# Query, key and value loads in partition halves, and attention products in 64x64 tiles, in a fused linear-attention and expert kernel

## The chip, the cores and the metric

The kernel runs on one core of a Trainium2 chip. The metric is the time of one execution on the device in microseconds (us), shorter is better. A core has a matrix engine (TensorE, "PE" in the profile, with its weight loads as "PEld"), VectorE ("DVE"), ScalarE ("ACT"), GpSimd ("POOL") and SyncE ("SP"), which here only issues transfers. Each engine runs its own instructions in order and waits on semaphores for the others. Data comes from main memory (HBM) by DMA into SBUF, which has 128 partitions; TensorE writes its products into PSUM, eight banks of 2 KB in each partition.

## The reference

Inputs are q, k and v of shape (4, 8, 768, 64): 4 batches, 8 heads, 768 tokens, 64 channels; a decay `lam` for each head; and the weights of an expert layer. All are float32.

```python
def _attn_ref(q, k, v, lam):
    block = 64
    ...
    Dmask = np.where(rel >= 0, lam[:, None, None] ** rel[None, :, :], 0.0)
    ...
    for b in range(nb):
        ...
        intra = np.einsum('bhic,bhjc->bhij', qb, kb) * Dmask[None]
        intra = np.einsum('bhij,bhjd->bhid', intra, vb)
        inter = np.einsum('bhid,bhde->bhie', qb * lam_pow[None], kv_state)
        out[:, :, sl] = intra + inter
        ...
        kv_state = lam_block[None, :, None, None] * kv_state + np.einsum('bhsd,bhse->bhde', kb_dec, vb)
    return out.astype(np.float32)

def _moe_ref(x, w_in, w_out, alpha):
    h = x @ w_in
    s = np.sin(alpha * h)
    g = h + s * s / (alpha + 1e-09)
    return (g @ w_out).astype(np.float32)
```

The attention's output, with the heads side by side, is the expert layer's x: 3072 tokens of 512 features. `w_in` is 512 x 2048 and `w_out` is 2048 x 512. Decay makes this linear attention: a token sees the tokens of its own block through masked scores, and all earlier ones of its batch through a state of 64 x 64 for each head.

## The kernel before, in words

**A planner.** The kernel doesn't write its instructions directly. Each step is given to `op(...)` with an engine (or a choice of engines), a guessed duration, and the names of the buffers that it reads and writes. `_Plan` puts the steps into an order of time by those guesses: SP's steps stay in the order given, TensorE's may be moved within a window of 40 steps, the others go to whichever engine would be done first. It then emits every engine's instructions with semaphore waits. `P.lead` moves a step ahead in that order. So the text sets the dependences and roughly the order, and the guessed durations set the rest.

**Blocks and chunks.** Tokens go in blocks of 128, which are 6 to a batch (`NB`) and 24 in all (`NBLK`). Four blocks make a chunk of 512 tokens (`TCH`), and there are 6 chunks.

**Attention of a block.** `load_q` brings q of two blocks (two tokens a run, 512 bytes), `load_kv` brings k and v of one block (one token a run, 256 bytes); all loads go through `load` (L340) on SP's queue. They are float32, with the 128 tokens of a block on the 128 partitions. `scale_block` multiplies q and k by powers of the decay (`Lq`, `Lk`; L459 and L466, mostly on POOL) into `qk2`, and copies v to bfloat16 (`v2`, L468). `piece_Q` and `piece_T` transpose q and k on TensorE for the first 12 blocks (`TD = 12`; L501 and L483), with copies out of PSUM into `qkT`; later blocks are transposed by a DMA on SP's queue (L474). `part_S` makes the scores in 64x64 tiles of the array (L536), and DVE multiplies them by the mask into `Sm` (L545). `part_O` adds two things in one PSUM bank: the carried state `Zc` times q, in 64x64 tiles (L590), and v times `Sm`, 128 tokens deep in 128x64 tiles (L597); its copy into `xT` (L606) is the transposed input of the expert layer. `part_Z` adds k times v into the state, also 128 deep (L561), in a bank of its own (`ZB`) that gathers through a batch; a copy to bfloat16 follows (L569). `run` joins such parts into one step of TensorE, and `piece_G` joins the scores of one block with the output and state of the block before.

**Expert layer.** `unit_A` makes 128 of the 2048 hidden features for a chunk, with four products of 128x512 (L645); ACT takes the sine (L655), POOL or ACT squares it (L660 or L659), and DVE adds it up into `gT` (L662). `unit_A2` does the same for two groups of 128 features and half a chunk (L679 to L697). `unit_B` makes a quarter of the sum over the hidden features for 128 tokens, with four products (L710); the last quarter is followed by a copy (L723) and a store (L725). The first quarter of `w_in` comes in float32 over SP's queue (`ws`) and is cast by DVE (L389); the other three and all of `w_out` come over GpSimd's queue with a cast in the transfer (L376 and L395 call `load`). The first of these waits for the last k of the first four blocks (`last["k32", 3]`); block 4's q waits for the weight load `last["w1", 2]`.

**Order.** Blocks 0 to 3 are done first, in pieces that are written out one by one. TensorE has little else then, and `spin` fills its gaps with products that nobody reads. Chunk 0's units A follow, then a written-out mixture of pieces of blocks 4 to 11, units B of chunk 0 and units A of chunk 1. From chunk 2 on a loop puts a unit A of chunk c beside a unit B of chunk c-1 and a joint attention run at five or four places of the sixteen.

Of the kernel before, what the change touches and what calls it, by code (L numbers as in the profile page):

```python
# [243 lines left out]
def bass_lightning_attn__then__act_snake_kernel(  # L244
# [34 lines left out]
    with es:  # L279
# [18 lines left out]
        q32 = ring("q32", RL // 2, [128, H, 2, D], F32)  # L298
        k32 = ring("k32", RL, [128, H, D], F32)
        v32 = ring("v32", RL, [128, H, D], F32)  # L300
        qk2 = sb("qk2", [128, R2, 2 * H, D], BF16)
        v2 = ring("v2", R2, [128, H, D], BF16)
        qkT = sb("qkT", [128, RT, 8, 128], BF16)
        Sm = ring("Sm", 2, [128, 8, 128], BF16)
        Zc = ring("Zc", 2, [128, 4, D], BF16)
        mask = sb("mask", [128, 8, 128], BF16)
        maskf = sb("maskf", [128, 128], F32)
        ident = sb("ident", [128, 128], BF16)
        identf = sb("identf", [128, 128], F32)
        lam_bc = sb("lam_bc", [128, H], F32)  # L310
        lnlam = sb("lnlam", [128, H], F32)
        E_i = sb("E_i", [128, 2 * NB, H], I32)
        E_f = sb("E_f", [128, 2 * NB, H], F32)
        lnL = sb("lnL", [128, 2 * NB, H], F32)
        Lq = sb("Lq", [128, NB, H], F32)
        Lk = sb("Lk", [128, NB, H], F32)
# [11 lines left out]
        def _(_unused_eng):  # L328
# [4 lines left out]
            op = P.op  # L333
            P.EARLY = 20.0, 0.3
# [8 lines left out]
            def load_q(s, after=()):  # L343


                b, n, j = s // NB, s % NB, s // 2 % (RL // 2)
                for lo, hi in ((0, 4), (4, H)) if s < 4 else ((0, H),):
                    last["q32", s] = load(
                        q32[j][:, lo:hi, :, :].rearrange("p h t d -> p h (t d)"),
                        q[b, lo:hi, n * BL:(n + 2) * BL, :].rearrange("h (p t) d -> p h (t d)", t=2),  # L350
                        [("q32", j, a) for a in range(lo // 4, hi // 4)],
                        (0.9 if s == 0 else 1.1 if s < 4 else 2.3), f"q32{j}" + (str(lo) if s < 4 else ""),
                        lat=2.7, after=after, runs=8 * (hi - lo),
                    )

            def load_kv(s, which="kv"):
                b, n, j = s // NB, s % NB, s % RL
                for nm, src, dst in (("k32", k, k32), ("v32", v, v32)):
                    if nm[0] in which:
                        last[nm, s] = load(  # L360
                            dst[j][:, :, :],
                            src[b, :, n * BL:(n + 1) * BL, :].rearrange("h p d -> p h d"),
                            (nm, j), 1.1, f"{nm}{j}", lat=2.7,
                        )

            def load_pair(s):
                load_q(s)
                load_kv(s)
                load_kv(s + 1)
# [16 lines left out]
            def cast_w1_first():  # L386
                for lo in (0, 256):
                    op("DVE",
                       lambda e, lo=lo: (e.copy if e is nc.scalar else e.tensor_copy)(  # L389
                           w1[:, :, lo:lo + 256], ws[:, :, lo:lo + 256]), 0.7, [("ws", lo)], [("w1", lo // 256)])  # L390

            def load_w2(i, after):
# [7 lines left out]
            load(lam_bc[:, :], bass.AP(lam.tensor, 0, [[0, 128], [1, H]]), "lam", 0.1, "lam", "ACT", runs=1)  # L400
            load(alphaT[:, :], bass.AP(moe_alpha.tensor, 0, [[128, NM], [1, 128]]), "alphaT", 0.1, "alphaT", "ACT", lat=4.9, runs=1)
            load_q(0)
            load_kv(0, "k")
            load_kv(1, "k")
            load_kv(0, "v")
            load_kv(1, "v")
            load_q(2)
            load_kv(2, "k")
            load_kv(3, "k")
            load_kv(2, "v")  # L410
            load_kv(3, "v")

            op("POOL", lambda e: e.iota(E_i[:, 0:NB, :], [[256, NB // 2], [1, 2], [0, H]], base=0,
                                        channel_multiplier=2), 0.6, writes=["E_i"])
            op("POOL", lambda e: e.iota(E_i[:, NB:2 * NB, :], [[128, NB], [0, H]], base=0, channel_multiplier=1),
               0.6, writes=["E_k"])
            op("POOL", lambda e: e.tensor_copy(E_f[:, :, :], E_i[:, :, :]), 0.3, ["E_i", "E_k"], ["E_f"])
# [7 lines left out]
                out=maskf[:, :], in_=maskf[:, :], pattern=[[1, 2], [2, 64]], compare_op=ALU.is_ge,  # L425
                fill=0.0, base=0, channel_multiplier=-1), 0.5, ["maskf"], ["maskf"])
            op("DVE", lambda e: e.tensor_copy(mask[:, :, :], bass.AP(maskf, 0, [[128, 128], [0, 8], [1, 128]])),
               0.8, ["maskf"], ["mask"])

            op("ACT", lambda e: e.activation(lnlam[:, :], lam_bc[:, :], ACTF.Ln), 1.5, ["lam"], ["lnlam"])  # L430
            lnlam_b = bass.AP(lnlam, 0, [[H, 128], [0, 2 * NB], [1, H]])
            op("DVE", lambda e: e.tensor_tensor(lnL[:, :, :], E_f[:, :, :], lnlam_b, ALU.mult), 0.2,
               ["E_f", "lnlam"], ["lnL"])
            op("ACT", lambda e: e.activation(Lq[:, :, :], lnL[:, 0:NB, :], ACTF.Exp), 0.3, ["lnL"], ["Lq"])
            op("ACT", lambda e: e.activation(Lk[:, :, :], lnL[:, NB:2 * NB, :], ACTF.Exp, scale=-1.0), 0.3,
# [10 lines left out]
            def QE(s, a):  # L446
                return "DVE" if (s, a) in () else "POOL"

# [4 lines left out]
            def scale_block(s):  # L453
                n, jl, j = s % NB, s % RL, s % R2
                lk = bass.AP(Lk, n * H, [[NB * H, 128], [1, H], [0, D]])
                jq = s // 2 % (RL // 2)
                for a in range(2) if s % 2 == 0 else ():
                    ported(op(QE(s, a),
                       lambda e, a=a: e.tensor_tensor(  # L459
                           qk2[:, j:j + 2, 4 * a:4 * a + 4, :],  # L460
                           q32[jq][:, 4 * a:4 * a + 4, :, :].rearrange("p h t d -> p t h d"),
                           bass.AP(Lq, n * H + 4 * a, [[NB * H, 128], [H, 2], [1, 4], [0, D]]), ALU.mult),
                       1.05 if QE(s, a) == "POOL" else 0.7,
                       [("q32", jq, a), "Lq"], [("q2", j, a), ("q2", j + 1, a)]))
                ported(op("DVE" if s in (0,1) else "POOL",
                   lambda e: e.tensor_tensor(qk2[:, j, H:2 * H, :], k32[jl][:, :, :], lk, ALU.mult), 0.7 if s in (0,1) else 1.05,  # L466
                   [("k32", jl), "Lk"], [("k2", j)]))
                op((("ACT", 0.62, 0.0), ("POOL", 1.05, 0.3)) if s > 11 else "ACT", lambda e: (e.copy if e is nc.scalar else e.tensor_copy)(v2[j][:, :, :], v32[jl][:, :, :]), 0.62,  # L468
                   [("v32", jl)], [("v2", j)])

            def piece_T(s, tb):
# [8 lines left out]
                def mm(e):  # L480
                    ins = None
                    for jp in range(4):
                        ins = e.transpose(tp[:, jp, :], qk2[:, j, H + 2 * jp:H + 2 * jp + 2, :], ident[:, :])  # L483
# [25 lines left out]
            def run(*parts, after=()):  # L509
# [4 lines left out]
                def mm(e):  # L514
                    ins = None
                    for p in parts:
                        ins = p[0](e)
# [386 lines left out]
```

## Time and profile before

| | us |
|---|---|
| median of 3 runs | 223.47 (223.21 to 226.68) |
| span of the profiled execution | 221.6 |
| TensorE busy | 205.4 |
| ACT busy | 154.1 |
| DVE busy | 119.5 |
| POOL busy | 89.2 |

The span reaches from the first to the last instruction of the core; the time of a run holds some 1.9 us more than that span. TensorE's granted clock is full (1.00) in all of it. Matmuls are pipelined: a 128x512 product is listed with 379 ns, of which 216 pass until the next one starts.

The largest groups, with busy time and the mean of one:

| line, engine, what | count | us | ns each |
|---|---|---|---|
| L710 PE, expert output | 381 | 90.9 | 370 |
| L645 PE, expert hidden, 512 tokens | 290 | 73.2 | 379 |
| L679 PE, expert hidden, 256 tokens | 176 | 22.3 | 273 |
| L536 PE, scores | 384 | 10.3 | 229 |
| L597 PE, v times scores | 192 | 10.2 | 229 |
| L590 PE, state times q | 160 | 8.0 | 218 |
| L561 PE, state update | 160 | 6.1 | 201 |
| L545 DVE, mask | 24 | 29.2 | 1222 |
| L459 POOL, scale of q | 24 | 25.0 | 1062 |
| L466 POOL, scale of k | 22 | 22.9 | 1044 |

By queue, SP's moved 76,880 packets with 24.25 MB, GpSimd's 3,696 with 3.67 MB, and ACT's 3,056 with 5.13 MB. The loads of k and of v are 24 each of 256 KB; those of q are 10 of 512 KB and 4 of 256 KB.

### The profile page before, as it was taken

To read this page: it belongs to the slowest core of one execution; us is meant where nothing else is said; L and a number is where in the kernel's file an instruction comes from. 1 tells how busy PE (TensorE), PEld (TensorE's weight loads), DVE (VectorE), ACT (ScalarE), POOL (GpSimd) and SP (SyncE) were. 2 spreads that over 40 slices of the span, in tenths; PEclk is the share of its full clock that TensorE was granted. 3 is DMA by queue.
4 is the path that set the end of the run, shared out by engine and by line. 5 is a ranking of instruction groups with operands and counts; after the bars stand their busy time and mean duration, and the time that the engine had idled before them with its cause. 6 is when DMAs were issued, how large, how long until landed. Compare 5 with 4: busy or idle time off the path is not lost.

```text
span 221.6 us, 4485 instructions
## 1 busy us (share of the span) xinstructions
PE 205.4 (93%) x1850; PEld 111.1 (50%) x1877; DVE 119.5 (54%) x179; ACT 154.1 (70%) x272; POOL 89.2 (40%) x98
## 2 busy tenths in 40 slices
PE   4687998899899998999999999999999999999995
PEld 1365433456576775545445444545545444444444
DVE  2687676254688867666545464645465544445100
ACT  3644995347697995879788877776777677778211
POOL 2485765344895985945550733011001011110100
PEclk9999999999999999999999999999999999999999
DMA  5999999999999999999999950110110011101212
GB/s 131 234 232 273 207 212 210 204 239 239 214 263 282 240 165 243 203 270 188 276 219 239 216 124 18 50 47 3 47 47 30 20 47 47 50 0 47 76 68 98
DMA packets 83653, 33.35 MB, mean 150 GB/s; under 512 B 63520, under 2 KB 80688, under 8 KB 83632
## 3 DMA queue, kind: packets, MB, share of 16 engines
q1 hardware_dynamic: 76880, 24.25, 54.0%
q0 software_dynamic: 3696, 3.67, 9.9%
q10 hardware_dynamic: 3056, 5.13, 6.4%
q8 instruction: 15, 0.25, 0.5%
q14 instruction: 6, 0.05, 0.1%
HBM read 27.28 MB, written 6.29 MB: 151 GB/s over the span
## 4 chain that ended last, share of the span: by engine, by line
PE 60%; DMA 18%; SPq 12%; POOL 4%; ACT 3%; issue 2%; DVE 1%
PE bank L710 29%; PE bank L645 23%; SPq L340 12%; DMA v<-in_v_dram 8%; DMA w<-in_moe_w_in_dram 4%; DMA q<-in_q_dram 3%; PE bank L679 3%; DMA k<-in_k_dram 3%; PE bank L597 2%; PE bank L536 2%; PE bank L590 1%; POOL qk L466 1%; POOL qk L459 1%; POOL u L694 1%; DVE gT L697 1%
## 5 line engine op out<-in xcount | busy, mean ns | idle before, releaser
L710 PE MATMUL bank<-w,gT 128*128 128x512 bf16 (+1 forms) x381 | 90.9, 370 | 2.2 <-issue 1.7
L662 DVE SCALAR_TENSOR_TENSOR gT<-u,rinv,bank 128x512 bf16<-128x512 bf16 x74 | 54.6, 746 | 54.1 <-ACT u L659 34.5
L645 PE MATMUL bank<-xT,w 128*128 128x512 bf16 x290 | 73.2, 379 | 0.9 <-DVE gT L662 0.4
L655 ACT ACTIVATE t<-bank,alpha 128x512 bf16<-128x512 f32 x74 | 50.5, 686 | 24.4 <-PE bank L645 24.4
L710 PEld LDWEIGHTS bank<-w,gT 128*128 128x128 bf16 x400 | 37.7, 98 | 39.5
L660 POOL TENSOR_TENSOR u<-t 128x512 bf16<-128x512 bf16 x21 | 21.8, 1041 | 82.0 <-ACT t L655 81.1
L645 PEld LDWEIGHTS bank<-xT,w 128*128 128x128 bf16 x296 | 28.5, 98 | 34.6 <-DVE gT L662 0.8
L545 DVE TENSOR_TENSOR Sm<-bank,mask 128x1024 bf16<-128x1024 f32 x24 | 29.2, 1222 | 9.8 <-PE bank L561 7.1
L659 ACT ACTIVATE u<-t 128x512 bf16<-128x512 bf16 x53 | 33.1, 628 | 1.6
L459 POOL TENSOR_TENSOR qk<-q,Lq 128x512 bf16<-128x512 f32 x24 | 25.0, 1062 | 19.6 <-DMA q<-in_q_dram 15.2
L466 POOL TENSOR_TENSOR qk<-k,Lk 128x512 bf16<-128x512 f32 x22 | 22.9, 1044 | 7.6 <-DMA k<-in_k_dram 7.5
L679 PE MATMUL bank<-xT,w 128*128 128x256 bf16 x176 | 22.3, 273 | 2.7 <-DVE gT L697 2.0
L723 ACT COPY osb<-bank 128x512 f32<-128x512 f32 (+1 forms) x25 | 14.2, 569 | 14.7 <-PE bank L710 14.6
L697 DVE SCALAR_TENSOR_TENSOR gT<-u,rinv,bank 128x256 bf16<-128x256 bf16 x44 | 19.0, 476 | 7.8 <-POOL u L694 4.3
L689 ACT ACTIVATE t<-bank,alpha 128x256 bf16<-128x256 f32 x44 | 18.5, 472 | 3.5 <-PE bank L679 2.9
L679 PEld LDWEIGHTS bank<-xT,w 128*128 128x128 bf16 x176 | 16.2, 98 | 6.3 <-DVE gT L697 3.4
L468 ACT CAST v<-v 128x512 bf16<-128x512 f32 x20 | 12.2, 615 | 8.8 <-DMA v<-in_v_dram 8.6
L606 ACT CAST xT<-bank 128x512 bf16<-128x512 f32 (+1 forms) x18 | 12.9, 715 | 2.8 <-PE bank L561 1.4
L694 POOL TENSOR_TENSOR u<-t 128x512 bf16<-128x512 bf16 x11 | 11.3, 1039 | 5.7 <-ACT t L689 5.6
L536 PEld LDWEIGHTS bank<-qkT 64*64 64x64 bf16 x384 | 6.5, 110 | 8.4 <-issue 3.2
L536 PE MATMUL bank<-qkT 64*64 64x128 bf16 x384 | 10.3, 229 | 0.5 <-ACT qkT L506 0.3
L597 PE MATMUL bank<-Sm,v 128*64 128x128 bf16 x192 | 10.2, 229 | 0.5 <-DVE Sm L545 0.5
(50 smaller groups left out, 102.6 us busy)
## 6 DMA issues: line engine op xcount, KB each, us to landing
k<-in_k_dram SPq DMA_DIRECT2D x24, 256.0 KB, 5.6
v<-in_v_dram SPq DMA_DIRECT2D x24, 256.0 KB, 5.5
q<-in_q_dram SPq DMA_DIRECT2D x10, 512.0 KB, 5.5
out_dram<-osb ACTq DMA_DIRECT2D x19, 256.0 KB, 2.1
w<-in_moe_w_out_dram POOLq DMA_DIRECT2D x4, 512.0 KB, 13.3
w<-in_moe_w_in_dram POOLq DMA_DIRECT2D x3, 512.0 KB, 9.3
q<-in_q_dram SPq DMA_DIRECT2D x4, 256.0 KB, 4.5
ws<-in_moe_w_in_dram SPq DMA_DIRECT2D x2, 512.0 KB, 6.6
```

What stands on the lines that cost most here:

```text
L340: return op(eng, lambda e: e.dma_start(dst, src), dur, dma=sem, lat=lat, after=after, issue=issue, runs=runs, writes=key if isinstance(key ...
L459: lambda e, a=a: e.tensor_tensor(qk2[:, j:j + 2, 4 * a:4 * a + 4, :], q32[jq][:, 4 * a:4 * a + 4, :, :].rearrange("p h t d -> p t h d"), b ...
L466: lambda e: e.tensor_tensor(qk2[:, j, H:2 * H, :], k32[jl][:, :, :], lk, ALU.mult), 0.7 if s in (0,1) else 1.05,
L536: ins = e.matmul(ps[(b0, b1)[h]][w, 128 * jp:128 * (jp + 1)].rearrange("p (t x) -> p t x", x=64), qkT[r, jt, 4 + jp, w], qkT[r, jq:jq + 2, ...
L545: op("DVE", lambda e: e.tensor_tensor(Sm[s % 2][:, :, :], banks[:, 512 * b0:512 * b0 + 1024].rearrange("p (c i) -> p c i", i=128), mask[:, ...
L645: ins = e.matmul(ps[hb][:, c0:c1], w1[:, kc, 128 * m:128 * (m + 1)], xT[x][:, kc, c0:c1], start=(kc == 0 and c0 == lo), stop=(kc == NKC - ...
L655: op("ACT", lambda e: e.activation(t16[ju][:, w], ps[hb][:, w], ACTF.Sin, scale=alpha[:, m:m + 1]), 0.69 * f, [bank(hb), "alpha"], [("t16" ...
L659: lambda e: (e.activation(u16[ju][:, w], t16[ju][:, w], ACTF.Square) if e is nc.scalar else e.tensor_tensor(u16[ju][:, w], t16[ju][:, w], ...
L660: e.tensor_tensor(u16[ju][:, w], t16[ju][:, w], t16[ju][:, w], ALU.mult)), 0,
L662: op("DVE", lambda e: e.scalar_tensor_tensor(out=gT[g][:, m, w], in0=u16[ju][:, w], scalar=rinv[:, m:m + 1], in1=ps[hb][:, w], op0=ALU.mul ...
L679: ins = e.matmul(ps[hb][:, 256 * i:256 * i + 256], w1[:, kc, 128 * (m + i):128 * (m + i + 1)], xT[x][:, kc, lo:lo + 256], start=(kc == 0 a ...
L710: ins = e.matmul(ps[ob][:, w], gT[g][:, m, 128 * s4:128 * (s4 + 1)], w2[:, m, w], start=(m == 0), stop=(m == NM - 1),)
```

## The change

q, k and v of a block are loaded alike now. `load_x` makes six transfers of 128 KB a block: for each of the three, heads 0 to 3 go to partitions 0 to 63 and heads 4 to 7 to partitions 64 to 127, with two neighbouring tokens in one run of 512 bytes. So a partition holds a pair of tokens for four heads. The factors, the mask and the layouts of `qk2`, `v2` and `Sm` follow that. Products over the tokens of a block are 64 deep now and come in twos (even and odd tokens), so v times scores has 16 products for 8, and the state update 16 for 8; scores and state times q keep 16 and 8. All are in 64x64 tiles. The new `run` puts the scores of a block and the output and state of the block before into one step, dealt out over the four tiles by a guess of 56 and 32 ns a product. Products of both row halves add into the same bank; between those of the one and of the other stands a wait of TensorE on a semaphore of its own (`turn`), with scores placed ahead of it. The output takes two half banks: one is the second half of the state's bank (`ZB`), which DVE therefore sets to zero after each copy (`WIPE`). Transposes on TensorE take q and k of one block into one bank with one copy out.

Besides: the first weight load on GpSimd's queue waits for the last v of block 3; half of the cast of `ws` is on ACT; the first four units A each do half a chunk; the banks are dealt out anew; blocks 0 to 3 and 4 to 12 have a new written-out order, in which no output run stands alone before the last block; and the joint runs of the later chunks stand at places 2, 6, 10 and 13.

```diff
-            def load_q(s, after=()):
...
-            def load_kv(s, which="kv"):
...
+            def load_x(s, which="qkv", after=()):
...
+                b, n, j = s // NB, s % NB, s % RL
+                for x in which:
+                    for r in range(2):
+                        last[x, s] = load(
+                            x32[x][j][half(r), :, :, :].rearrange("p h t d -> p h (t d)"),
+                            {"q": q, "k": k, "v": v}[x][b, 4 * r:4 * r + 4, n * BL:(n + 1) * BL, :].rearrange(
+                                "h (p t) d -> p h (t d)", t=2),
+                            (x + "32", j, r), 0.47, f"{x}32{j}{r}", lat=2.7, after=after, runs=16,
                         )
...
-            load(lam_bc[:, :], bass.AP(lam.tensor, 0, [[0, 128], [1, H]]), "lam", 0.1, "lam", "ACT", runs=1)
+            for r in range(2):
+                load(lam_bc[half(r), :], bass.AP(lam.tensor, 4 * r, [[0, 64], [1, 4]]), ("lam", r), 0.1, f"lam{r}", "ACT", runs=1)
...
+            for s in range(4):
+                load_x(s)
...
+            def run(S=None, O=None, Z=None, b0=3, ob=2, ob2=None, parted=False, after=()):
...
+                if O is not None:
+                    for t in range(2):
+                        for r, u, w in RUW:
+                            first.append((r, w, 56, (obs[r], w), out_of(r, u, w),
+                                          v2[O % R2][half(r), 2 * u + w, t, :], Sm[O % 2][half(r), u, 2 * w + t, :]))
+                if O is not None and O % NB:
+                    for r, u, w in RUW:
+                        (first if r == u else then).append(
+                            (u, w, 56, (obs[r], w), out_of(r, u, w).rearrange("p (t x) -> p t x", t=2),
+                             Zc[O % 2][half(u), 2 * r + w, :], q_of(O, r, u, w)))
+                if Z is not None:
+                    for t in range(2):
+                        for r, u, w in RUW:
+                            (first if r else then).append(
+                                (r, u, 32, (ZB, u), ps[ZB][half(u), 64 * (2 * r + w):64 * (2 * r + w) + 64],
+                                 qk2[half(r), Z % R2, 1, 2 * w + t, u, :], v2[Z % R2][half(r), 2 * u + w, t, :]))
...
+                full = max(lanes.values()) + 110
...
+                    for i, (_, _, _, key, d, w, x) in enumerate(first + early + then):
+                        if first and then and i == len(first + early):
+                            e.wait_ge(turn, turns[0])
+                        ins = e.matmul(d, w, x, start=key not in begun, stop=True, skip_group_check=True)
+                        begun.add(key)
+                        if first and then and i == len(first) - 1:
+                            turns[0] += 1
+                            ins.then_inc(turn, 1)
...
+                    if ob2 is None:
+                        op(WIPE, lambda e: e.memset(ps[ZB][:, 256:512], 0.0), 0, [("xT", c % RX, i4, 2)], [bank(ZB)])
...
             for i in range(1, 4):
-                load_w1(i, [last["k32", 3]])
+                load_w1(i, [last["v", 3]])
...
+            FIRST = ("T4 G4 T5 G5 BBB BBB T6 G6 BBB T7 BBB G7 "
+                     "0 0 T8 0 0 G8 B 1 1 T9 1 B 1 G9 A T10 B A G10 A B A T11 A A G11 A A G12")
...
-                    if block <= NBLK and m in ((2, 6, 8, 11, 13) if c == 2 else (2, 7, 10, 13)):
...
+                    if block <= NBLK and m in (2, 6, 10, 13):
+                        attend("G", block)
                         block += 1
```

More of the change, by code (lines that the diff above doesn't have):

```diff
@@ new lines, in piece_T, with mm @@
+                for i, x in ((1, "k"), (0, "q")) if s == 0 else ((0, "q"), (1, "k")):
+                    def mm(e, i=i):
+                        ins = None
+                        for w in range(4):
+                            ins = e.transpose(tp[:, 4 * i + w, :], qk2[:, j, i, w, :, :], ident[:, :])
+                        return ins
+                    op("PE", mm, 0.3, [(x + "2", j), "ident"], [bank(tb)])
+                op((("DVE", 0.7, 0.0), ("ACT", 1.1, 0.0)),
+                   lambda e: (e.copy if e is nc.scalar else e.tensor_copy)(qkT[:, jt, :, :], tp),
+                   0, [bank(tb)], [("qT", jt), ("kT", jt)])
@@ L628, in _, with piece_G @@
+            def piece_G(s, t, ob=2):
+                run(S=s, O=t, Z=t, ob=ob)
             seen = [0]
@@ L847, in _ @@
+            assert ai == 16 and not stores, (ai, bi)
+            block = TD + 1
             for c in range(2, NCH):
```

476 lines of the change are left out of this document (196 added, 280 removed).

## The prediction

> **What bounds the kernel now.** I read the busy table and the slices first.
>
> ```profile
> PE 205.4 (93%) x1850; PEld 111.1 (50%) x1877; DVE 119.5 (54%) x179; ACT 154.1 (70%) x272; POOL 89.2 (40%) x98
> ...
> PE   4687998899899998999999999999999999999995
> ...
> DMA  5999999999999999999999950110110011101212
> ```
>
> TensorE is the bound from the fourth slice on, and the DMA engines are full for the first 115 us. The stretches say where the one waits for the other (columns: stretch, length, then busy us and instructions of each engine, clock, DMA share, GB/s).
>
> ```profile
> 0.00:20.70 20.70, 13.76 (x188) 8.11 (x190) 12.92 (x22) 10.61 (x18) 11.78 (x20) 1.00 1.03 218
> 20.70:45.00 24.30, 22.23 (x123) 10.63 (x127) 14.05 (x23) 15.93 (x27) 13.32 (x14) 1.00 1.16 207
> 45.00:87.00 42.00, 39.61 (x543) 27.79 (x548) 30.27 (x54) 32.00 (x69) 29.69 (x31) 1.00 1.09 235
> 87.00:125.00 38.00, 36.99 (x356) 18.93 (x361) 22.05 (x31) 31.68 (x56) 21.15 (x22) 1.00 1.20 234
> 125.00:204.00 79.00, 77.89 (x565) 37.52 (x573) 38.74 (x51) 60.09 (x96) 12.26 (x12) 1.00 0.15 47
> ```
>
> The expert products start only at 20.69; behind 87 us TensorE never rests, so there only fewer TensorE cycles help. Between, it idles a little. The chain of waits gives the reason for the late start: the issues on SP's queue, then the landing of k, then the expert weights.
>
> ```profile
> 0.81 0.45 SPq L340
> ...
> 1.32 0.48 SPq L340
> ...
> 9.14 5.70 DMA k<-in_k_dram
> ...
> 14.90 1.04 POOL qk L466
> 15.95 0.88 POOL w L340
> 16.82 9.34 DMA w<-in_moe_w_in_dram
> ```
>
> TensorE's timeline shows one joint attention run of now, and three stalls of the middle stretch.
>
> ```profile
> 38.92 0.40 PE L501 MATMUL bank<-ident,qk 128*128 128x128 bf16 x4 [0.75 <-POOL qk L459]
> ...
> 43.80 0.40 PE L483 MATMUL bank<-ident,qk 128*128 128x128 bf16 x4 [0.81 <-POOL qk L466]
> ...
> 59.54 1.05 PE L679 MATMUL bank<-xT,w 128*128 128x256 bf16 x8 [0.90 <-DVE gT L697]
> ...
> 98.85 0.42 PE L536 MATMUL bank<-qkT 64*64 64x128 bf16 x16
> 99.10 0.39 PE L590 MATMUL bank<-qkT,Zc 64*64 64x128 bf16 x8
> 99.42 0.41 PE L597 MATMUL bank<-Sm,v 128*64 128x128 bf16 x8
> 99.67 0.29 PE L561 MATMUL bank<-v,qk 128*64 128x64 bf16 x8
> 100.12 1.67 PE L645 MATMUL bank<-xT,w 128*128 128x512 bf16 x7 [0.16 <-issue]
> ```
>
> The profiled span is 221.6 us; the median of the runs, 223.47, is 1.9 above it. I sum against the span and add 1.9.
>
> **Loads at the start.** The completion records of the first four blocks give the pace of 256 KB: q (512 B runs) lands 0.95 to 0.98 us behind its forerunner (4.95 to 5.93, 11.48 to 12.43); k and v (256 B runs) 1.16 on average (5.93 to 10.58 for four, 12.43 to 17.07 for four). After, all have 512 B runs, but as twice as many transfers of 128 KB, each into half the partitions. No transfer of the trace is of that kind. Bounds: 0.95 per 256 KB, if halves run as whole ones of equal runs, and 1.9, if a half takes as long as a whole one. SP sets a floor: starts of unblocked issues lie 0.51 to 0.54 apart (0.81, 1.32, 1.85, 2.40), so 1.04 for two. I take p = 0.98, the nearest row. With 5.93 for the first two, the last load lands at 5.93 + 10p = 15.7, not 17.07.
>
> What waits for it moves: the first GpSimd weight load now waits for the last v, not the last k. Before, it is issued at 15.89, its first packet comes at 18.71, its 512 packets run at 412 per 2 us (2.5), and it is complete at 23.62, 1.8 behind its last packet. After, that is 15.7 + 0.1 + 2.8 + 2.5 + 1.8 = 22.9, and the product that reads it, now at 24.52, starts there: **-1.6 us** (10p - 11.4; +7.6 at p = 1.9). The first products need only ws (behind the last v by some 2 us, and 0.7 for the cast) and could start near 18.5; but they then stand before this weight load, so it sets the gain, not they. The extra lam load on ACT's queue (0.44) and the half-range DVE edits lie ahead of 7 us, when POOL waits for the factors anyway: nothing, at most 0.5.
>
> **Attention on TensorE.** From matmul starts, a joint run now: enters (drain 0.093 and a slow first group, 0.024), 16 score products in groups of four lanes, 56 ns a group, 0.224; carried state, 8 on two lanes, 0.224; change to 128 rows, 0.114; 8 products with v, 0.224; state update, 8 at 31 ns a pair, 0.124; leaves, 0.112. Sum 1.14, and the gap in the weight stream is 1.147. After: 56 products, all on four lanes: 0.224 + 0.112 + 0.224 + 0.124 = 0.684, one entry and one leave 0.229, sum 0.913. To that the new semaphore: TensorE waits for its own last product of the first group before it adds from the other row half. That product takes 0.216 to its end, consumers start 0.04 later (the first state copy at 12.31, its product ends at 12.27), and scores cover 0.112 behind its own 0.056: 0.09 open, and 0.024 to refill; lanes of unequal length cost up to 0.1 more. Queued behind it are the rest of the run and the next expert product. I take 1.06 to 1.09: -0.05 to -0.08 for each of 19 joint runs, -1.0. Three more visits to TensorE fall away (lone runs for blocks 5, 7, 11 and 6, 8, 12 become joint), 0.25 each: -0.7. **-1.7 us**. Bounds: no stall at all, 0.91, gives -5.2; a stall of 0.35 gives +3.
>
> [...]
>
> **Stalls from 20.7 to 87.** Gaps between matmul starts beyond streaming time and drains sum to 4.3 us: 0.91 at 37.8 and 0.97 at 42.6 (block 4's q, then k), 1.07 at 58.5, 0.46 at 68.1, 0.93 at 84.1. While the w_out loads run, one q packet goes for one weight packet (283 each per 2 us). q of blocks 4 and 5 now takes 1024 such turns, and k 1024 more: k lands at 42.64. After, block 4's q and k are 1024 turns in all, so both are there when q is now (37.76): the second stall goes, and half of the first. The 58.5 stall is ACT held by a v cast until 57.41; with blocks 0.3 us cheaper it shrinks. Against it: a lone output run no longer exists, so block 5's output waits for block 6's load, block 7's for block 8's; what covers that are 16 expert-output units of 0.86, which end about 50, when block 6 is there. Taken: **-2.1** (from -4 to +2).
>
> **Off the path.** Twenty memsets of 128x256 in PSUM on DVE, between 0.17 (128x128 memset) and 0.43 (copy from PSUM, same shape): 3 to 9 us, beside a DVE busy 38.7 of 79 late on; nothing. Without that cover up to 0.4 a run, 8 in all. Copy of the state now precedes the output copy (0.37 on ACT): hidden while runs lie 5 us apart. Transposed pairs come out of PSUM in one copy, 0.69 a block for 0.77. POOL scales as much as before. SP issues six loads a block, 3.1 us, ahead of each transpose (2 to 3.6): under 7 of TensorE's 8 a block. All nothing.
>
> Sum: -1.6 - 1.7 - 2.1 = -5.4: span 216.2, time **218.1**.
>
> **Rivals.** [...]
>
> [...] At p = 1.6 the start costs +4.6, and blocks 5 to 8 land 4.8 apart instead of 3.1 (50.66 to 66.30 for five), three of them +5, with the joint runs waiting for the next block and no units left; -1.7 for attention: +7.9, 231.4. It passes +2% from p = 1.42, 0.71 per half.
>
> *The run isn't shorter*: products that start 20 ns apart instead of 12 (56 of them, +0.45 a run, 19 runs) turn -1.7 into +6.8: 226.6; a stall of 0.25 more gives 223. [...]
>
> **Numbers.** Forecast 0.45 (215 to 220.5; 0.42 of it under 219.0, which is -2%, about what a measurement can tell from no change), no faster loads 0.20 (0.02 faster, the rest within), slower loads 0.26 (0.24 over +2%), no shorter run 0.09 (0.06 within, 0.03 slower). Faster 0.44, within 0.29, slower 0.27. Range 215 to 229: it leaves out the worst half of the slower loads and 0.06 below.
>
> **What would show it.** Last v landing near 15.7 and products of w_in's second chunk at 22.9; 512 B packets near 30 ns; joint runs of 1.07; no idle at block 4's transposes. Wrong if q, k, v land over 1.15 us per 256 KB, if TensorE idles at block 6 or 8, or if a run exceeds 1.15.

## The result, and the profile after

The changed kernel takes 239.58 us (median of 4 runs, 236.31 to 240.18), the kernel before 223.43 beside it (223.21 to 226.68): a ratio of 1.064, 95% interval 1.057 to 1.072. By the medians it is 16 us slower, where 5.4 less were forecast, and lies outside the range. The ratio compares the faster runs alone (239.28 and 236.31 against 223.21 to 223.47), and by it the loss is 14.4 us. The profiled execution is the one of 240.18 us and has a span of 238.4 us. The busy row and three rows of the slices:

```profile
PE 213.7 (90%) x2214; PEld 109.6 (46%) x2214; DVE 123.2 (52%) x190; ACT 150.3 (63%) x260; POOL 95.9 (40%) x102
...
PE   5778899969957569996999999999999999999995
...
PEclk9965999999999999997999999999999999999999
DMA  4768999997676698697999889011101110111122
```

TensorE now has a long dip in slices 12 to 15, some 66 to 89 us, and two short stretches of less than full clock. The DMA engines, full for 115 us before, are no longer full at the start and in that dip. The stretches say it in numbers (columns as in the prediction):

```profile
0.00:20.70 20.70, 14.09 (x162) 6.90 (x162) 9.03 (x18) 7.93 (x13) 6.69 (x13) 0.84 0.61 168
...
45.00:87.00 42.00, 30.34 (x506) 18.62 (x503) 20.91 (x36) 21.34 (x44) 24.79 (x24) 1.00 0.82 206
87.00:125.00 38.00, 35.09 (x402) 17.85 (x403) 24.75 (x39) 28.10 (x52) 22.84 (x24) 0.96 0.86 198
```

In 45 to 87 us TensorE is busy 30.3 us in place of 39.6: 9.3 us less, where the span grew by 16.8 in all. The DMA share is 0.61 and 0.82 where it was 1.03 and 1.09. So something ahead of the DMA engines holds the loads back. The chain of waits at the start names it (start, length, what):

```profile
2.35 0.61 SPq L343
2.96 0.04 issue
3.00 0.62 SPq L343
3.62 0.04 issue
3.66 0.62 SPq L343
...
13.56 4.25 DMA q<-in_q_dram
17.88 1.05 POOL qk L444
```

SyncE issues one half every 0.66 us: 0.62 in the issue, 0.04 between. Before, the first issues were 0.45 and 0.48 long. Two halves take 1.32 us, so the six of a block take 3.96, and the 24 of blocks 0 to 3 fill SP's queue until 17.9 (one of them took 1.74). The queue's timeline shows the same in the middle (start, length of all, count at the end):

```profile
64.96 1.27 SPq L343 DMA_DIRECT2D v<-in_v_dram  x2
66.28 1.28 SPq L343 DMA_DIRECT2D q<-in_q_dram  x2
67.60 1.27 SPq L343 DMA_DIRECT2D k<-in_k_dram  x2
68.94 1.26 SPq L343 DMA_DIRECT2D v<-in_v_dram  x2
```

What waits for it is ScalarE, which works in order and stands at each cast of v (in brackets the idle time ahead, and what ended it):

```profile
20.74 0.62 ACT L450 CAST v<-v 128x512 bf16<-128x512 f32 x1 [3.75 <-DMA v<-in_v_dram]
...
68.63 0.62 ACT L450 CAST v<-v 128x512 bf16<-128x512 f32 x1 [1.60 <-DMA v<-in_v_dram]
...
72.97 0.62 ACT L450 CAST v<-v 128x512 bf16<-128x512 f32 x1 [2.12 <-DMA v<-in_v_dram]
...
77.06 0.62 ACT L450 CAST v<-v 128x512 bf16<-128x512 f32 x1 [1.50 <-DMA v<-in_v_dram]
```

Block 3's v is there at 20.7, 3.6 us later than before (17.1). In the middle the casts follow each other in 4.1 to 4.3 us, a little over the 3.96 of six issues. Behind each cast stand sines and copies, and TensorE waits for what comes of them:

```profile
67.63 1.05 PE L650 MATMUL bank<-xT,w 128*128 128x256 bf16 x8 [1.39 <-DVE gT L668]
...
70.21 0.62 PE L466 MATMUL bank<-ident,qk 128*128 128x128 bf16 x8 [1.53 <-ACT xT L587]
...
75.08 1.05 PE L650 MATMUL bank<-xT,w 128*128 128x256 bf16 x8 [1.55 <-DVE gT L668]
```

These casts stand far ahead of their use. Counted in the order of the blocks, the cast at 68.63 is that of block 10, and the mask step of block 10 runs only at 88.43 (before: 65.75 and 77.67).

### The profile page after: what moved, and what is told of

Read it like the earlier page. It is cut to its first block, busy times and chain, and to the rows that moved or that the text cites. A ratio compares the mean times of both kernels' runs of the same rounds, so it can differ in the third digit from the quotient of the medians.

```text
span 238.4 us, 5336 instructions
## 1 busy us (share of the span) xinstructions
PE 213.7 (90%) x2214; PEld 109.6 (46%) x2214; DVE 123.2 (52%) x190; ACT 150.3 (63%) x260; POOL 95.9 (40%) x102
## 4 chain that ended last, share of the span: by engine, by line
PE 62%; DMA 18%; SPq 9%; ACT 5%; POOL 2%; issue 2%; DVE 1%; ACTq 0%
PE bank L681 28%; PE bank L616 25%; DMA v<-in_v_dram 11%; SPq L343 8%; PE bank L549 5%; DMA q<-in_q_dram 4%; DMA k<-in_k_dram 2%; ACT v L450 2%; POOL qk L444 2%; PE bank L650 2%; PE bank L749 1%; ACT u L630 1%; SPq L456 1%; PE bank L466 1%; ACT osb L694 1%
## 5 line engine op out<-in xcount | busy, mean ns | idle before, releaser
L681 PE MATMUL bank<-w,gT 128*128 128x512 bf16 (+1 forms) x400 | 95.8, 373 | 0.0
L616 PE MATMUL bank<-xT,w 128*128 128x512 bf16 x320 | 80.9, 382 | 3.0 <-DVE gT L668 2.8
L616 PEld LDWEIGHTS bank<-xT,w 128*128 128x128 bf16 x320 | 30.9, 98 | 40.5 <-DVE gT L668 3.4
L444 POOL TENSOR_TENSOR qk<-q,Lq 128x512 bf16<-128x512 f32 x22 | 22.9, 1042 | 29.0 <-DMA q<-in_q_dram 28.8
L450 ACT CAST v<-v 128x512 bf16<-128x512 f32 x21 | 12.9, 615 | 33.4 <-DMA v<-in_v_dram 33.4
L444 POOL TENSOR_TENSOR qk<-k,Lk 128x512 bf16<-128x512 f32 x23 | 24.3, 1058 | 13.5 <-DMA k<-in_k_dram 6.5
L668 DVE SCALAR_TENSOR_TENSOR gT<-u,rinv,bank 128x256 bf16<-128x256 bf16 x32 | 13.6, 477 | 14.6 <-POOL u L665 9.0
L650 PE MATMUL bank<-xT,w 128*128 128x256 bf16 x128 | 15.7, 273 | 5.7 <-DVE gT L668 5.0
L466 PE MATMUL bank<-ident,qk 128*128 128x128 bf16 x96 | 9.3, 231 | 8.7 <-POOL qk L444 5.1
L549 PE MATMUL bank<-qkT 64*64 64x128 bf16 x384 | 15.1, 227 | 0.2 <-DVE qkT L471 0.2
L660 ACT ACTIVATE t<-bank,alpha 128x256 bf16<-128x256 f32 x32 | 13.3, 471 | 2.5 <-PE bank L650 2.4
L549 PE MATMUL bank<-v,qk 64*64 64x64 bf16 x320 | 12.0, 196 | 0.7 <-ACT Zc L577 0.3
L466 PEld LDWEIGHTS bank<-ident,qk 128*128 128x128 bf16 x96 | 5.9, 102 | 13.3 <-POOL qk L444 7.1
L587 DVE CAST xT<-bank 128x512 bf16<-128x512 f32 (+1 forms) x10 | 7.0, 702 | 9.3 <-PE bank L549 8.6
```

Of the source, the lines that this page charges most:

```text
L444: ported(op(eng, lambda e, x=x, i=i, L=L: e.tensor_tensor(qk2[:, j, i, :, :, :].rearrange("p w u d -> p u w d"), bass.AP(x32[x][jl], 0, [[ ...
L549: ins = e.matmul(d, w, x, start=key not in begun, stop=True, skip_group_check=True)
L616: ins = e.matmul(ps[hb][:, c0:c1], w1[:, kc, 128 * m:128 * (m + 1)], xT[x][:, kc, c0:c1], start=(kc == 0 and c0 == lo), stop=(kc == NKC - ...
L650: ins = e.matmul(ps[hb][:, 256 * i:256 * i + 256], w1[:, kc, 128 * (m + i):128 * (m + i + 1)], xT[x][:, kc, lo:lo + 256], start=(kc == 0 a ...
L681: ins = e.matmul(ps[ob][:, w], gT[g][:, m, 128 * s4:128 * (s4 + 1)], w2[:, m, w], start=(m == 0), stop=(m == NM - 1),)
```

## The experiments

Three theories were on record before the first run. Theory 1: the number of SyncE's issues sets the pace. Theory 2: it is that a load writes half of the partitions. Theory 3: the planner guesses 0.4 us for an issue, so its order is made for loads that come earlier than they do, and ScalarE stands at casts that nobody needs yet. Kernels that start with `a` are changed from after, those with `b` from before.

### The loads alone, put into the kernel before

`b_six`: before, with its loads cut by heads into six a block, 128 KB and all 128 partitions each.

```diff
-for lo, hi in ((0, 4), (4, H)) if s < 4 else ((0, H),):
+for lo, hi in ((0, 2), (2, 4), (4, 6), (6, H)):
...
-    last[nm, s] = load(dst[j][:, :, :], src[b, :, ...], (nm, j), 1.1, ...)
+    for lo in (0, 4):
+        last[nm, s] = load(dst[j][:, lo:lo + 4, :], src[b, lo:lo + 4, ...], (nm, j, lo), 0.55, ...)
```

> The kernel before, with its loads of q, k and v cut by heads into six transfers a block instead of 2.5; all still go to 128 partitions, with the same bytes and the same runs. Theory 1 (SP's issues set the pace: each takes 0.62 us and 0.04 of gap, so six are 3.96 a block): the last v of block 3 lands near 20 instead of 17.1, ACT waits for v casts far longer than the 8.6 us of before, and the time rises by 5 to 12 us, to 228 to 236. Theory 2 (writing half the partitions is what slows the loads): nothing here writes halves, so the loads land as before and the time is 222 to 226.

Measured: 230.33 us (229.16 to 231.99) against 223.99, ratio 1.029 (1.023 to 1.035). The time is inside what theory 1 said, its reason is not: block 3's last v landed at 18.4 us, not near 20, and the median issue took 0.47 us (q) and 0.51 (k, v), not 0.62. The planner had made a new order too, so the pace alone was not yet shown.

`b_sixp`: the same, planned for 0.66 us an issue.

```diff
-def load(..., issue=0.4, runs=64):
+def load(..., issue=0.66, runs=64):
```

> Before with the loads cut by heads into six a block, as in the earlier run of that kind, and now with the order planned for 0.66 us a load. If that run's loss of 6.3 us against before came from an order, and a filling with warming products, made for earlier loads: 224 to 227, clock 1.00. If it came from the pace of the loads itself: 228 to 231.

Measured: 229.63 (227.41 to 230.44) against 224.39, ratio 1.021 (1.012 to 1.029): the guess was worth little here. By the expectation, 228 to 231 meant that the pace itself made the loss; the last pair below speaks against that.

`b_halfp`: as `b_sixp`, but each load writes 64 partitions with twice the heads.

```diff
-for lo in (0, 4):
-    last[nm, s] = load(dst[j][:, lo:lo + 4, :], src[b, lo:lo + 4, n * BL:(n + 1) * BL, :]...
+for r in (0, 1):
+    last[nm, s] = load(dst[j][64 * r:64 * r + 64, :, :], src[b, :, n * BL + 64 * r:n * BL + 64 * r + 64, :]...
```

> Before with six loads a block planned for 0.66 us each, as in the run of 229.6 us, but each load of 64 partitions and twice the heads in place of 128 partitions; every engine but SyncE keeps that kernel's instructions and order, and the packets are as long. Theory 2 (a transfer that writes half the partitions is slower): v of blocks 0 to 3 lands over 1 us later, and the time is over 232. Theories 1 and 3 (the count of the loads, not their shape): 228 to 231.

Measured: 240.55 (237.95 to 241.12) against 223.54, ratio 1.071 (1.064 to 1.079): 10.9 us over the kernel that differs in the shape of the loads alone. Theories 1 and 3 had said 228 to 231. They fall as the main cause, and theory 2 takes their place, though not in the way it was meant: SyncE's median issue was 0.62 (q) and 0.635 us (k, v), against 0.47 and 0.51 in `b_sixp`.

Because `b_sixp` and `b_halfp` have another order than before, the last pair keeps before's order on every engine: the pieces of a load are one step of the plan.

```diff
-lambda e: e.dma_start(dst, src)
+lambda e: [e.dma_start(a, c) for a, c in cut(dst, src, sem)]
...
+# b_xheads                                   # b_xhalf
+[(dst[:, a:a + h, :], src[:, a:a + h, :])    [(dst[64 * r:64 * r + 64, a:a + h, :], src[64 * r:64 * r + 64, a:a + h, :])
+ for a in range(0, dst.shape[1], h)]          for a in range(0, dst.shape[1], h) for r in range(2)]
```

> Before with each load of q, k and v put out as transfers of 128 KB that write 64 partitions (two in place of one for 256 KB, four for 512 KB), all still one step of the plan: every engine has before's instructions in before's order, and only SyncE issues more. Theory 2 as the run of 240.5 us now reads it (SyncE is held 0.62 us by a load into 64 partitions against 0.51 into 128, so 1.32 us per 256 KB, 3.96 a block): SyncE's last load of block 3 ends at 16.5 to 18 us, its loads stand back to back in 45 to 75 us, and the time is 234 to 242. If that run's loss was made by its order: 224 to 230.

> The same with transfers of 128 KB that write all 128 partitions (cut by heads): before's order on every engine, as many transfers as in the kernel beside it. Theory 2 as above (0.51 us and 0.03 between, 1.07 per 256 KB, 3.2 a block, about what the transfers need): the last load of block 3 is issued by 14 us and the time is 224 to 228, at least 7 us under the kernel with halves. Theory 1 (the count of the transfers alone): both kernels take the same time.

Measured, against 224.34 us: `b_xheads` 226.40 (226.29 to 226.59), ratio 1.011 (1.007 to 1.015); `b_xhalf` 237.04 (235.87 to 238.84), ratio 1.061 (1.053 to 1.069). SyncE's timeline and two stretches of `b_xheads`:

```profile
0.81 1.98 SPq L347 DMA_DIRECT2D q<-in_q_dram  x4
2.83 2.12 SPq L347 DMA_DIRECT2D k<-in_k_dram  x4
...
11.70 2.19 SPq L347 DMA_DIRECT2D v<-in_v_dram  x4
```

```profile
0.00:20.00 20.00, 13.56 (x187) 7.55 (x189) 13.19 (x21) 10.42 (x18) 11.31 (x20) 1.00 0.90 217
...
45.00:87.00 42.00, 37.74 (x526) 26.22 (x528) 28.24 (x50) 30.21 (x66) 29.25 (x31) 1.00 0.89 218
```

And the same of `b_xhalf`:

```profile
0.81 2.71 SPq L348 DMA_DIRECT2D q<-in_q_dram  x4
3.56 2.65 SPq L348 DMA_DIRECT2D k<-in_k_dram  x4
...
14.33 2.67 SPq L348 DMA_DIRECT2D v<-in_v_dram  x4
```

```profile
0.00:20.00 20.00, 13.82 (x152) 7.60 (x154) 10.49 (x19) 8.73 (x14) 9.39 (x18) 1.00 0.71 170
...
45.00:87.00 42.00, 36.28 (x459) 24.14 (x464) 25.65 (x45) 27.05 (x58) 24.35 (x25) 0.96 0.79 198
```

Twenty-four loads are issued by 13.9 us in the one and by 17.0 in the other, with as many bytes and transfers. The count costs 2.1 us (less than 2% of before); that each writes 64 partitions costs 10.6 more. Against theory 1's "both kernels take the same time", that decides it. The loss grows through the stages that wait for loads: `b_xhalf` does the mask step of block 4 at 49.06 us and `b_xheads` at 45.35, that of block 11 at 89.27 and 82.67, that of block 15 at 116.78 and 107.32; from there the distance stays (block 23: 179.35 and 169.90). `b_xhalf` has before's attention products, and is 12.7 of after's 16 us slower (by the ratios, 1.061 of 1.064).

The pair also corrects `b_sixp`: the same cut by heads cost 5.2 us there and 2.1 here, so some 3 us of that loss came with its order and not with the loads.

### Is it the issue, or the transfer?

`a_act4`: after, the second halves of blocks 0 to 3 issued on ScalarE's queue.

```diff
-f"{x}32{j}{r}", lat=2.7, ...
+f"{x}32{j}{r}", "ACT" if r and s < 4 else "SP", lat=2.7, ...
```

> The changed kernel, with the second half of each load of blocks 0 to 3 issued on ACT's queue, which is nearly idle then; the halves, bytes and runs are unchanged. Theory 1 (issues): twelve issues a queue are 7.9 us, so DMA sets the pace at 0.95 to 1.1 us per 256 KB; the last v of block 3 lands at 15.5 to 17.5 instead of 20.7 and the time falls by 3 to 5 us. Theory 2 (half the partitions): the last v still lands at 19 or later, and the time falls by less than 1.5 us.

Measured: 241.84 (241.47 to 242.89), ratio 1.081 (1.077 to 1.085): no gain. The issues stand in front of ScalarE's first logarithm, which runs at 12.1 us where it ran at 4.7, and the decay factors are late. The row of waits that says so (us in all, times, longest), and two stretches of 3 us, in the first of which both queues were issuing halves:

```profile
POOL qk L444 <- ACT Lk L423: 12.7, 1, 12.7
```

```profile
6.00:9.00 3.00, 3.00 (x10) 1.04 (x9) 0.35 (x2) 0.00 (x0) 0.00 (x0) 1.00 1.01 258
9.00:12.00 3.00, 0.77 (x4) 0.16 (x2) 0.00 (x0) 1.19 (x1) 0.00 (x0) 1.00 1.19 264
```

As a test of the time it fails, and by its own mark it even speaks for theory 2: block 3's last v landed at 19.0 us (after: 20.7), "19 or later". But SyncE had gone on to the weights `ws` at 9.0 us, and their 1 MB moved beside ScalarE's last halves. The rows answer the question better. Until then most issues held each queue 0.62 to 0.64 us, both at once, and in 6 to 9 us the halves moved at 258 GB/s, 0.51 us each; after moved 198 there and before's whole loads 214 (in 6 to 12 us: 261, 197 and 239). Nor did a packet take longer in a half: of the 256-byte packets that began in 3 to 9 us the median took 18 ns in `b_xhalf` and in `b_xheads`. So in `a_act4` the transfers went faster than the one half every 0.66 us of after, and what held after's to that pace was its one issuing queue.

`a_pool`: order planned for 0.66 us, and five second halves of blocks 2 and 3 issued by GpSimd. Beyond the lines shown, the second half of each load now comes before the first in the order.

```diff
+aside = r and (s == 3 or s == 2 and x != "q")
-f"{x}32{j}{r}", lat=2.7, after=after, runs=16,
+f"{x}32{j}{r}" + "p" * bool(aside), "POOL" if aside else "SP", lat=2.7, after=aux if aside else after, runs=16, issue=0.85 if aside else 0.66,
```

> After with the order planned for 0.66 us a load, and five second halves (k and v of block 2; q, k and v of block 3) issued by GpSimd, which is idle from 1.9 to 6.7 us, in place of SyncE. Theory 1 (SyncE's issue of 0.66 us a load sets when the first blocks land): SyncE's last half of block 3 is issued at 13.4 instead of 16.6, v of block 3 is cast by 17.5 instead of 20.4, the first second-quarter product starts by 26.5 instead of 29.2, and the time falls by 2 to 5 us from the 233.7 of the kernel planned so without the move: 229 to 232. Theory 2 (halves land slowly, whoever issues them): the last v lands as late as before, 233 to 235.

Measured: 232.74 (231.79 to 234.48), the same as `a_plan` below. SyncE was done with block 3 at 13.5 us, as expected, but GpSimd's early transfers came ahead of block 0's own: its k was scaled at 8.7 in place of 6.7, and block 3's v cast at 19.7, not by 17.5. Inconclusive.

`a_mid`: order planned for 0.66 us, and the second halves of k and v from block 4 on issued by ScalarE.

```diff
+f"{x}32{j}{r}", "ACT" if r and s > 3 and x != "q" else "SP", ...
```

> After with the order planned for 0.66 us a load, and the second halves of k and v of blocks 4 on issued on ScalarE's queue. Theory 1 carried to the middle (there SyncE issues six loads of 0.66 back to back, 3.96 us a block, and ScalarE's casts of v stand 4.0 to 4.3 us apart): with four issues on SyncE (2.6 us a block) the casts come 3.3 us apart, TensorE's idle time in 45 to 87 falls from 8.6 to 3 to 5 us, and the time from 233.7 to 229 to 231. Rival (the transfers, or ScalarE itself at 0.64 us an issue, bound that stage): the casts stay 4 us apart or ScalarE's products come later, 233 to 236.

Measured: 236.67 (236.46 to 236.88), 3 us over `a_plan`. In the middle it did half of what theory 1 said: the DMA share rises to 1.21, and casts come 3.4 to 3.5 us apart, but TensorE's idle time falls only from 8.6 to 7.8 us, not to 3 to 5:

```profile
63.77 0.62 ACT L451 CAST v<-v 128x512 bf16<-128x512 f32 x1 [2.93 <-DMA v<-in_v_dram]
...
67.29 0.64 ACT L451 CAST v<-v 128x512 bf16<-128x512 f32 x1
...
70.69 0.62 ACT L451 CAST v<-v 128x512 bf16<-128x512 f32 x1 [0.77 <-DMA v<-in_v_dram]
```

```profile
45.00:87.00 42.00, 34.23 (x517) 21.34 (x516) 25.98 (x43) 19.53 (x42) 27.45 (x28) 0.92 1.21 236
```

But ScalarE issued blocks 4 and 5 already among the first blocks' work, and the first expert product came at 27.3 in place of 23.7. The casts' pace in the middle follows the issues; a faster pace, paid for on ScalarE, gained nothing.

### The order

`a_plan`: after, with 0.66 us guessed for a load's issue and 1.35 for a transpose's.

```diff
-def load(..., issue=0.4, runs=64):
+def load(..., issue=0.66, runs=64):
-dma=f"qkT{jt}", runs=16)
+dma=f"qkT{jt}", runs=16, issue=1.35)
```

> The changed kernel, with nothing changed but two guesses in the planner: 0.66 us for the issue of a load instead of 0.4, and 1.35 for that of a transpose. Theory 3 (the loss in the middle comes from an order written for loads that come earlier than they do, so ACT stands before v casts with the expert's sines behind it): ACT's waits for v fall from 33.4 us to under 15, and the time falls by 5 to 11 us. Theory 1 alone (the pace of the issues starves TensorE whatever the order): ACT's waits may fall, but TensorE idles as much and the time stays within 2 us.

Measured: 233.72 (231.81 to 235.58), ratio 1.041 (1.032 to 1.051): 5.9 us under after by the medians and 5.2 by the ratios, with the same transfers and the same work in another order. ScalarE's waits for v fall only from 33.4 to 25.2 us, not to under 15 as expected, so the gain is there and its stated reason is half right. TensorE is busy 33.4 of the 42 us. The longest stall left is of the kind that theory 3 names, a copy behind a cast:

```profile
70.79 0.62 PE L466 MATMUL bank<-ident,qk 128*128 128x128 bf16 x8 [3.45 <-ACT xT L587]
```

`a_vlate`: `a_plan`, with v from block 4 on taken to land 3 us later, so that its casts move back in ScalarE's order.

```diff
-lat=2.7
+lat=5.7 if x == "v" and s > 3 else 2.7
```

> After with the order planned for 0.66 us a load, and with v's loads from block 4 on taken to land 3 us later than the others; loads and their order on SyncE are those of the kernel planned for 0.66 alone (233.7 us). Only the orders written for TensorE, ScalarE, VectorE and GpSimd change: ScalarE's casts of v move behind copies and sines. Theory 3 (ScalarE stands at a cast of a block that nobody needs yet, and TensorE then waits for ScalarE's xT copy, 3.5 us at 67 to 71 us in that kernel): ScalarE's waits for v fall from 25.2 us to under 12, TensorE's idle time in 45 to 87 from 8.6 to under 6, and the time by 2 to 4 us, to 229.5 to 231.5. Theory 1 alone (blocks come 4 us apart and TensorE has no other work there): the idle time stays, under other names, and the time too, 233 to 235.

Measured: 234.72 (233.37 to 237.08). The waits for v fall to 17.5 us, not under 12, and the time doesn't fall. TensorE is idle for 8.8 of the 42 us, as long as in `a_plan`, now mostly for GpSimd's scaled q and k. That is what theory 1 alone had foretold. It doesn't prove that the pace is too slow: an order that asks for blocks too early would stall in the same way.

`a_best`: four edits together, in the hope of a version faster than both (planned for 0.66, v late, v's second halves on ScalarE, weights triggered by block 3's k).

```diff
+f"{x}32{j}{r}", "ACT" if r and s > 3 and x == "v" else "SP", lat=5.7 if x == "v" and s > 3 else 2.7,
+after=[*after, last["v", 3]] if r and s > 3 and x == "v" else after, ...
 ...
-load_w1(i, [last["v", 3]])
+load_w1(i, [last["k", 3]])
```

> After with four edits together: order planned for 0.66 us a load, v of block 4 on taken to land 3 us later, its second half issued on ScalarE's queue once v of block 3 has been issued and landed, and the loads of w1 and w2 waiting for block 3's k again. SyncE then issues five loads a block, 3.3 us. If pace and order in the middle make the loss, each counted once: below the kernel with the first two edits by 1 to 4 us, 226 to 230. If ScalarE's issue (0.64 us) holds its own work up as much as SyncE gains: no better than that kernel.

Measured: 238.70 (238.52 to 240.12): no better than `a_plan`, `a_vlate`, `a_mid` or `a_trig`. No kernel of this study beats the one before.

### Two smaller parts

`a_trig`: after, with the first weight loads waiting for block 3's k again.

```diff
-load_w1(i, [last["v", 3]])
+load_w1(i, [last["k", 3]])
-load_w2(i, [last["v", 3]] if i < 2 ...
+load_w2(i, [last["k", 3]] if i < 2 ...
```

> The changed kernel, with the first GpSimd weight loads waiting for the last k of block 3 again, as before the change. If the later trigger costs at the start, as the prediction had it: the weights land some 2 us earlier (24.6 instead of 26.55) and the time falls by 1 to 2.5 us. If the attention of blocks 2 and 3 sets the start of the expert products now, the time stays within 1 us.

Measured: 237.77 (237.11 to 238.65), 1.8 us under after, which itself varies by 3.9; the ratios, 1.062 and 1.064, are the same. GpSimd issues the weights at 19.8 in place of 21.0, and the first load is complete at 25.4 in place of 26.6. But the first product that reads it starts at 30.9 where after's starts at 30.7. So the trigger doesn't set the start of the second quarter; the attention of blocks 2 and 3 does, as the other expectation had it. Only the later loads gain, since block 4's q waits for a weight load: its v is cast at 44.7 in place of 46.7.

`a_spin`: after's clock stood at half from 14.2 to 24.5 us; here five more of the products that nobody reads fill TensorE's gaps ahead of that.

```diff
-n = int((t - at) / 0.4)
+n = int((t - at) / 0.4 + (0.8 if at > 8 else 0))
```

> After, with five more of the warming products (128x512, 0.39 us each at full clock) put into the real gaps of TensorE between 9 and 18 us; every other instruction and its order is after's. Theory 4 (the half clock of 14.2 to 24.5 us in after follows the 3.4 us window from 10.8 us in which TensorE was busy 0.64, and is itself a part of the loss): granted clock 1.00 from 7 to 45 us and the time 2 to 4 us below after's 239.6, since products other than the warming ones spent some 3.0 us more in that stretch than at full clock. Theories 1 and 3 alone (pace of the loads, order): nothing gained, 239 to 241, since the loads land as before and five products more are in the way.

Measured: 238.88 (238.49 to 239.94). The clock stayed full from 7.7 to 48.6 us, and the time hardly moved. The test is not clean, for the clock was at half for 3.4 us from 48.6 and again from 69.1. But block 4's mask step came 0.9 us earlier than in after and block 11's 1.3, and `a_plan`, with full clock throughout its profiled execution, is still 9 to 10 us over before. So the half clock at the start is no main cause.

## Why the prediction was wrong

**The loads at the start (-1.6).** This step failed, and its pace failed at one row: "SP sets a floor: starts of unblocked issues lie 0.51 to 0.54 apart (0.81, 1.32, 1.85, 2.40), so 1.04 for two." Those four are loads into 128 partitions. For loads cut by heads the figure would have been right: `b_xheads` has 24 in 13.1 us, 0.55 each. In after a load into 64 partitions held the queue 0.62 us, with its gap 0.66, so 1.32 per 256 KB and not 0.98. The last v landed at 20.7, not at 15.7. The prediction had said that "no transfer of the trace is of that kind", and then took SP's price from another kind all the same. The named condition for being wrong, over 1.15 per 256 KB, came true. (The packets were as forecast: those of 512 bytes that began in 3 to 9 us took 27 ns in the median, before and after.)

**The pace's price.** By the prediction's own formula, 10p - 11.4, a pace of 1.32 makes +1.8 us, and its rival of slower loads passed +2% only from 1.42. Both were too mild. The formula also has a reading wrong: before, the 512 packets of the first weight load take 3.1 us from the first to the last (18.71 to 21.84), not 2.5, so p = 0.98 makes -1.0.

And the weight load "sets the gain, not they" failed. The second-quarter product came at 30.7, where 22.9 was forecast and before's came at 24.5, but its weights were there at 26.6, and `a_trig`, with weights 1.1 us earlier, starts no earlier. Before it stand the attention of blocks 2 and 3 and units of half a chunk, which the chain of waits shows behind block 3's q:

```profile
24.98 1.85 PE bank L650 x16
26.83 0.43 PE bank L549 x20
...
27.61 0.46 DVE xT L587
...
28.20 1.91 PE bank L650 x16
...
30.72 1.40 PE bank L616 x6
```

Little of these 6.1 us lasts: block 4's mask step runs at 47.22, where before's ran at 45.46.

**Off the path, and the stalls (-2.1).** "SP issues six loads a block, 3.1 us, ... under 7 of TensorE's 8 a block. All nothing." This holds the larger half of the loss. The block takes 3.96 us of SP's queue, and the sentence set 3.1 against the later stream alone, for all of the kernel. In 45 to 87 us TensorE is 9.3 us less busy, where the term for the stalls had -2.1, and ScalarE waits 33.4 us in all at casts of v, where before's waited 8.6. From block 4's mask step to block 11's the delay grows from 1.8 to 11.4 us (before 81.03, after 92.42). Another 5.5 us are lost up to block 15's (104.60 and 120.48): ScalarE stands at a cast until 106.48, and the clock is at half from 109.8 to 113.2.

A mean pace doesn't explain this. Before's mask steps of blocks 4 to 11 lie 5.1 us apart, more than 3.96, and its own casts of blocks 4 to 12 come 4.1 us apart (43.51 to 76.01), after's 3.8 (46.68 to 77.06). What is shown is that loads land later than the written order expects and that engines which work in order stand and wait for them: halves alone do it to before's order (`b_xhalf`), and other guesses alone take 5 to 6 us back (`a_plan`). How the stage's loss splits between late loads and order stays open.

**Attention (-1.7).** Right for the joint run, in mechanism and size. From matmul starts: after's joint runs begin at 119.41 and 125.65 with 24 expert products of 0.2158 between, so a run costs 6.24 - 5.18 = 1.06 us; before, 118.06 to 127.84 with 40, 1.15. Forecast were 1.06 to 1.09. The three lone runs that fall away (-0.7 of the term) were not measured. The timeline of the first (each run of equal products begins a row):

```profile
118.45 1.03 PE L616 MATMUL bank<-xT,w 128*128 128x512 bf16 x4
119.41 0.42 PE L549 MATMUL bank<-Sm,v 64*64 64x128 bf16 x16
...
120.36 1.04 PE L681 MATMUL bank<-w,gT 128*128 128x512 bf16 x4
```

Fifty-six products lie between 119.41 and 120.36, 17 ns each; the rival with products 20 ns apart did not come.

**What was not in the sum.** The planner's guess of 0.4 us for an issue was worth little with loads into 128 partitions (`b_six` and `b_sixp`), and cost 5 to 6 us when two halves took 1.32 (`a_plan`). As an estimate from the runs: 2.1 for the count, 10.6 for the halves, 5.9 for the order and -1.7 for attention make 16.9, where 16.2 were measured. The terms come from different kernels, so that agreement is no proof of the split: by the ratios the same terms make 17.2 of 14.4 us, and the 10.6 were measured with an order that was not made for halves either, so the two terms may overlap.

**The rivals.** *Slower loads*, the case of p = 1.6, had the right side: two halves took 1.32 us, over the 0.98 of the sum. But what bound them was the issuing queue, held 0.62 us by each half, and not the transfers: with two queues issuing, a half went every 0.51 us (`a_act4`, 6 to 9 us). *No faster loads* has 0.20 in the chances; no run shows halves from one queue at the 1.16 us per 256 KB of before's k and v, and after's took 1.32.

## What to carry over

Price a transfer's issue by a row of the same shape: 128 KB in 512-byte runs held SyncE's queue 0.62 us here when they went into 64 partitions and 0.47 when into 128, and the time of one issue times the count per block is a pace that has to be set against each stage, and against the order that waits for the loads there. When loads are changed in a kernel with an order made from guesses, change the guesses too. To learn what a change of loads costs, put the pieces into one step of the order that is there, and let nothing else move.

## What was not expected of the hardware

- SyncE was held 0.47 us by 128 KB into 128 partitions with 512 B runs, 0.51 with 256 B runs (both in `b_sixp`), 0.62 into 64 partitions with 512 B runs, 0.635 with 256 B runs (both in `b_halfp`). For 256 KB into 128 it was 0.45 to 0.50 in the first three loads of before, and 0.58 for the k at 84.1 us. So here partitions mattered more than bytes or the number of packets; why is open. ScalarE's queue took 0.64 for a half in `a_act4`, GpSimd's 0.63 in `a_pool`.
- Two queues issuing halves at once reached 258 GB/s in 6 to 9 us of `a_act4`; one alone moved 195 to 202 in 3 to 15 us of after.
- TensorE's granted clock fell to half in after from 14.2 to 24.5 and from 109.8 to 113.2 us, behind 3.4 us with TensorE 0.64 and 0.49 busy. `a_plan` had such stretches too (0.42 from 68.8 us) and kept the full clock, so that share alone doesn't decide it.
